# The last product of a chain of matrix products: weights instead of tokens held still in TensorE, and results turned by VectorE

## Chip, cores, metric

One core of a Trainium2 chip. The metric is the device time of one execution in microseconds (us), the median of three runs. A core has TensorE (matrix products, results to PSUM), VectorE, ScalarE and GpSimd (POOL) for elementwise work, SyncE (SP), which issues the DMAs here, and 16 DMA engines between the on-chip memory (SBUF) and the device memory.

## What is computed

Attention with keys and values pooled by 8, and then two blocks of two matrix products each, on 4608 tokens of width 512:

```python
x = attention(q, k, v)                       # 4608 x 512
h = x @ moe_w_in                             # 512 -> 2048
x = np.maximum(0.01 * h, h) @ moe_w_out      # 2048 -> 512
h = x @ moe2_w_in
neg, pos = h <= -1, h >= 1
g = np.where(pos, h, np.where(neg, 0.0, (h + 1) ** 2 / 4))
out = g @ moe2_w_out                         # 4608 x 512
```

Inputs are float32, the weights float64. Each product is made of three TensorE products of a high and a low part (hi x hi, lo x hi, hi x lo).

## The kernel before

There are four stages, one after the other. The first makes the attention and the first product (lines 588 to 590), the second the product with moe_w_out, the third the product with moe2_w_in (line 874), the fourth the product with moe2_w_out. The second and the fourth are two objects of one class, `Blocks`, with `layer` 0 and 1.

`Blocks` multiplies in the manner of Strassen and Winograd: tokens come in pairs of blocks ("pair r": 512 and 512 tokens, the last pair 256 and 256), the 2048 inner columns in two halves, the 512 output columns in two halves, and seven products of sums of blocks replace eight. `ORDER2` is the order of the seven. A **unit** is one of the seven products for one of eight slices f of the inner columns, so there are 5 x 7 x 8 = 280 units: 224 of pairs 0 to 3 and 56 of the last pair. `run` goes through them in order. For unit u it issues

- `unit(u)`: TensorE's matmuls. Layer 0 holds a 128x128 piece of the weights still and moves n tokens (n = 512, in the last pair 256) through it, six matmuls a unit; a result has output columns as its rows (partitions) and tokens along them. Layer 1 holds 128 tokens still and moves 256 columns of the weights, 3 n/128 matmuls a unit; a result has tokens as its rows;
- `hi(u+5)`, ScalarE's copy of the source to the high part (line 1093), and `lo(u+4)`, VectorE's subtraction for the low part (line 1098); the parts lie in six pairs of buffers in turn;
- `g_sum`: the sums of token blocks, on VectorE (line 1078) or, for odd f of the pairs 1 to 3, as an adding DMA issued by POOL (line 1076);
- `g_load`: SP's loads of the next pair (line 1059);
- two steps of `post`, which takes finished products out of PSUM: ScalarE's copies (`snap`, line 1224), VectorE's adds and subtractions (lines 1241 and 1232), POOL's adds (line 1247). A finished block of the result is put on the list `late` with the unit at which SP is to store it (`STORES_LATE` is 6 units on; others 2).

Every engine works through its own instructions in the order in which they were issued, and waits by semaphores. In layer 1 the output tiles of a long pair (`out_tile`) are three rooms, `spare[0]` to `spare[2]`, the fourth tile taking `spare[0]` again. A block of the result, tokens x 256 columns, is stored by one DMA in rows of 1 KB.

In the third stage the weights of the fourth are prepared: `w2_sums` (POOL, lines 785 to 788), `w2_split` (ScalarE line 616, VectorE lines 619 and 621) and a store to device memory.

## Time and profile before

| | |
|---|---|
| time, median of 3 runs | 1664.01 us (1663.68 to 1667.12) |
| profiled execution, its own time | 1663.9 us |
| its span, first to last instruction | 1661.9 us |
| TensorE busy | 1613.5 us, 97% of the span |
| VectorE busy | 1199.9 us, 72% |
| ScalarE busy | 979.3 us, 59% |
| POOL busy | 454.5 us, 27% |
| second stage: first and last matmul start | 576.9 and 929.8 us |
| fourth stage: first and last matmul start | 1291.0 and 1657.6 us |

The profile is of one execution, and the sums below are made against its own time. Busy time is an average over stages with different limits: what a change in one stage is worth is read from that stage, from the wait that ends last there. PE is TensorE, PEld its weight loads, DVE VectorE, ACT ScalarE. Matmuls overlap, so the time of one (the mean) is longer than the distance between two; the busy time of a group divided by its count is the distance.

### The profile page before, as it was taken

Reading aid. Unit: us, or ns where it says so; the run is one execution under the profiler, and the core shown is the slowest. Engines: PE = TensorE matmul, PEld = TensorE weight load, DVE = VectorE, ACT = ScalarE, POOL = GpSimd, SP = SyncE. Lnnn points to the kernel's source line nnn. Section 1 sums busy time; section 2 is a strip of 40 time slices with the busy share of each in tenths; the row PEclk is TensorE's granted clock in tenths of the full one; section 3 lists DMA queues with packets and bytes.
Section 4 is the critical chain, followed back from the end, with each engine's and each line's share of the span. In section 5 each row is a group of like instructions: output and inputs, shape, how many; then the busy total and the mean of one; then the engine's idle time right before and its main releaser. Section 6 shows DMA issues by size and latency. Waiting matters only on the chain.

```text
span 1661.9 us, 28512 instructions
## 1 busy us (share of the span) xinstructions
PE 1613.5 (97%) x9324; PEld 1446.6 (87%) x9324; DVE 1199.9 (72%) x2383; ACT 979.3 (59%) x2113; POOL 454.5 (27%) x572
## 2 busy tenths in 40 slices
PE   6899999999999999999999999999999999999999
PEld 4578787788788888888889999999999999999998
DVE  6858868877855198899898456775673876676767
ACT  4646655556555355666655578887886545454545
POOL 3424333342532003343441111222210013232210
PEclk9999999999999999999999999999999999999999
DMA  7647867678675798899959567557557987777731
GB/s 223 179 142 236 259 225 257 222 237 272 207 231 186 283 364 247 209 280 244 254 148 317 182 223 256 176 195 252 179 199 239 360 269 160 206 156 205 158 117 62
DMA packets 225363, 366.27 MB, mean 220 GB/s; under 512 B 26240, under 2 KB 104064, under 8 KB 225216
## 3 DMA queue, kind: packets, MB, share of 16 engines
q1 hardware_dynamic: 211392, 339.30, 61.3%
q0 software_dynamic: 13824, 25.17, 9.0%
q8 instruction: 73, 1.20, 0.3%
q14 instruction: 74, 0.61, 0.1%
HBM read 196.61 MB, written 142.61 MB: 204 GB/s over the span
## 4 chain that ended last, share of the span: by engine, by line
PE 80%; DVE 10%; ACT 3%; DMA 3%; issue 3%; POOL 1%; SPq 0%; DVEq 0%; ACTq 0%; POOLq 0%
PE u L1135 22%; PE u L1126 20%; PE Y L874 7%; PE h L588 6%; PE h L589 6%; PE h L590 6%; PE X L874 5%; PE V L874 4%; PE sc L432 1%; PE tm L491 1%; DVE vs L338 1%; DVE vr L359 1%; DMA g<-tV 1%; DMA wb0i<-in_moe_w_in_dram 1%; PE av L508 1%
## 5 line engine op out<-in xcount | busy, mean ns | idle before, releaser
L1093 ACT ACTIVATE m<-m 128x512 fp32r<-128x512 f32 (+1 forms) x560 | 328.2, 589 | 320.4 <-PE u L1135 146.8
L1098 DVE TENSOR_TENSOR m<-m,m 128x512 fp32r<-128x512 f32 (+1 forms) x560 | 385.9, 701 | 169.9 <-ACT m L1093 153.1
L1135 PE MATMUL u<-v,m 128*128 128x256 f32 x3024 | 365.1, 284 | 1.7 <-DVE m L1098 1.7
L1135 PEld LDWEIGHTS u<-v,m 128*128 128x128 f32 x3024 | 364.6, 193 | 2.2 <-DVE m L1098 2.1
L1126 PE MATMUL u<-m,v 128*128 128x512 f32 (+1 forms) x1680 | 349.5, 370 | 3.8 <-DVE m L1098 3.6
L1126 PEld LDWEIGHTS u<-m,v 128*128 128x128 f32 x1680 | 294.6, 189 | 58.7 <-DVE m L1098 6.0
L588 PE MATMUL h<-xh,w0i 128*128 128x512 f32 x448 | 184.0, 411 | 0.8 <-ACT t L596 0.8
L589 PE MATMUL h<-xl,w0i 128*128 128x512 f32 x448 | 177.2, 396 | 3.4 <-DVE xl L176 3.4
L590 PE MATMUL h<-xh,w0i 128*128 128x512 f32 x448 | 177.4, 396 | 0.0
L1247 POOL TENSOR_TENSOR o<-o,o 128x512 f32<-128x512 f32 x36 | 63.8, 1799 | 354.2 <-DVE o L1241 352.8
L596 ACT ACTIVATE t<-h 128x512 f32<-128x512 f32 x144 | 86.0, 597 | 122.3 <-PE h L590 67.5
L1078 DVE TENSOR_TENSOR m<-m,m 128x512 f32<-128x512 f32 (+1 forms) x224 | 141.0, 629 | 0.0
L1076 POOL DMA_DIRECT2D m<-m x96 | 84.0, 1036 | 136.4 <-DVE m L1098 108.5
L468 POOL TENSOR_TENSOR at<-at,r 128x32 f32<-128x32 f32 (+3 forms) x160 | 72.3, 473 | 154.9 <-DVE r L465 121.0
L588 PEld LDWEIGHTS h<-xh,w0i 128*128 128x128 f32 x448 | 85.5, 191 | 20.2 <-ACT t L596 1.6
L589 PEld LDWEIGHTS h<-xl,w0i 128*128 128x128 f32 x448 | 85.5, 191 | 19.7 <-DVE xl L176 4.2
L590 PEld LDWEIGHTS h<-xh,w0i 128*128 128x128 f32 x448 | 85.1, 190 | 18.8
L874 PE MATMUL Y<-xs,v 128*128 128x384 f32 x432 | 86.7, 336 | 3.9 <-DVE p L893 3.1
L874 PE MATMUL X<-xs,v 128*128 128x384 f32 x432 | 86.9, 335 | 0.0
L874 PE MATMUL V<-xs,v 128*128 128x384 f32 x432 | 86.5, 334 | 0.0
L874 PEld LDWEIGHTS Y<-xs,v 128*128 128x128 f32 x432 | 75.4, 188 | 6.2 <-DVE p L893 4.1
L874 PEld LDWEIGHTS X<-xs,v 128*128 128x128 f32 x432 | 76.3, 189 | 0.0
(261 smaller groups left out, 2678.9 us busy)
## 6 DMA issues: line engine op xcount, KB each, us to landing
m<-g SPq DMA_DIRECT2D x256, 256.0 KB
g<-t SPq DMA_DIRECT2D x144, 256.0 KB
m<-m POOLq DMA_DIRECT2D x96, 256.0 KB, 5.7
wf<-v0o SPq DMA_DIRECT2D x56, 256.0 KB
wi<-v1i SPq DMA_DIRECT2D x56, 256.0 KB
v<-wf SPq DMA_DIRECT2D x28, 512.0 KB
v<-wi SPq DMA_DIRECT2D x28, 512.0 KB
w2d<-w2o SPq DMA_DIRECT2D x56, 256.0 KB
```

The source lines that it names most:

```text
L468: nc.gpsimd.tensor_tensor(out=t, in0=t, in1=r[0:n].to_broadcast([n, 4, w]), op=ALU.mult)
L588: nc.tensor.matmul(ph, wh[:, c], xh, start=k == 0, stop=False)
L589: nc.tensor.matmul(ph, wh[:, c], xl, start=False, stop=False)
L590: nc.tensor.matmul(ph, wl[:, c], xh, start=False, stop=k == KT - 1)
L596: nc.scalar.activation(out=t, in_=h_t.pop(f), func=AF.Prelu, alpha=0.01)
L874: nc.tensor.matmul(ps, w[:, c], x[k, i], start=begin and k == n == 0, stop=k == 1 and n == 2, skip_group_check=True,)
L1076: nc.gpsimd.dma_start(out=t, in_=x, accum_op=ALU.add)
L1078: nc.vector.tensor_tensor(out=t, in0=x, in1=t, op=ALU.add)
L1093: nc.scalar.activation(out=self.s[u][0], in_=self.unit_source(u), func=AF.Copy)
L1098: nc.vector.tensor_tensor(out=lo, in0=self.unit_source(u), in1=hi, op=ALU.subtract)
L1126: nc.tensor.matmul(banks[b][:, at:at + n], w[:, c], x, start=fresh and at == 0 and i == 0, stop=end and i == 2, skip_group_check=True,)
L1135: nc.tensor.matmul(ps, a[:, c], w, start=fresh and tt % 2 == 0 and i == 0, stop=end and i == 2, skip_group_check=True,)
```

## The change

In layer 1 a unit now has the form of layer 0: a piece of the weights still, n tokens moving. The results come with output columns as rows, and have to be turned before they are stored. VectorE's transpose turns blocks of 32 x 32: block b of 32 tokens and the 32 rows 32a to 32a+31 become 32 rows of tokens. So that the blocks of all four products of a token put together 128 neighbouring output columns in each of the four groups of 32 partitions, the columns are shared out: column 4m + 2e + h of the result is row m of half e of block column h, and `w2_sums` and `w2_split` read the weights in that order (elements 16 bytes apart). `turned` turns a quarter, 256 tokens of one block column, by two instructions into the tile z, in steps of 16 bytes; after the second block column it issues four DMAs, one for each 32 partitions, in pieces of 512 bytes. z has one room, `spare[3]`. The table `TURN` says which quarters are turned when, in units after a block was finished. The fourth output tile takes `spare[1]`.

```diff
--- before.py
+++ after.py
@@ -32,6 +32,10 @@
 UNITS_AHEAD = 10
 EARLY = 12
 STORES_LATE = 6
+TURN = {
+    "r1": (), "r2": (("r1", 0, 2), ("r2", 0, 3), ("r1", 1, 6), ("r2", 1, 7)),
+    "q": (("q", 0, 5),), "c11": (("c11", 0, 0), ("q", 1, 4), ("c11", 1, 4)),
+}
 FIRST = [((2, 1), f) for f in (5, 6, 7)] + [((1, 1), f) for f in range(8)]

 SCORES1 = (-3, -1, 2, 3, 3, 5, 9, 10, 11, 11)
@@ -779,8 +783,10 @@

         def w2_sums(self, f):
             t = self.kept["w2"]
-            b11, b12, b21, b22 = t[:, 0, 0:256], t[:, 0, 256:], t[:, 1, 0:256], t[:, 1, 256:]
-            s = wpool.tile([P, 4, 256], F32, tag=self.spare[1], name=f"w2s{f}")
+            b11, b12, b21, b22 = (
+                t[:, r].rearrange("p (m e h) -> p h e m", e=2, h=2)[:, h] for r in range(2) for h in range(2)
+            )
+            s = wpool.tile([P, 4, 2, P], F32, tag=self.spare[1], name=f"w2s{f}")
             tt = nc.gpsimd.tensor_tensor
             tt(out=s[:, 0], in0=b12, in1=b11, op=ALU.subtract)
             tt(out=s[:, 1], in0=b22, in1=s[:, 0], op=ALU.subtract)
@@ -794,7 +800,8 @@
                     [P, 2, 2, 256], F32R, tag=self.spare[2 + pos // 2 % 2], name=f"w2o{f}_{pos}"
                 )
             t = self.kept["w2o"][:, pos % 2]
-            for _ in signed_split(t[:, 0], t[:, 1], self.kept["w2s"][ORDER2[pos]], ORDER2[pos] < 4):
+            hi, lo = (t[:, i].rearrange("p (e m) -> p e m", e=2) for i in range(2))
+            for _ in signed_split(hi, lo, self.kept["w2s"][ORDER2[pos]], ORDER2[pos] < 4):
                 pass
             nc.sync.dma_start(out=self.w2d[pos][:, f], in_=t.bitcast(F32))

@@ -1118,22 +1125,12 @@
             hi, lo = self.s.pop(u)
             wh, wl = self.w[pos, f]
             fresh, end = prod not in (2, 3) and f == 0, f == self.NJ - 1
-            if self.layer == 0:
-                for e in range(2):
-                    c = slice(e * P, (e + 1) * P)
-                    b, at = divmod(e * n, 512)
-                    for i, (x, w) in enumerate(((hi, wh), (lo, wh), (hi, wl))):
-                        nc.tensor.matmul(
-                            banks[b][:, at:at + n], w[:, c], x, start=fresh and at == 0 and i == 0, stop=end and i == 2,
-                            skip_group_check=True,
-                        )
-                return
-            for tt in range(n // P):
-                c = slice(tt * P, (tt + 1) * P)
-                ps = banks[tt // 2][:, 256 * (tt % 2):256 * (tt % 2) + 256]
-                for i, (a, w) in enumerate(((hi, wh), (hi, wl), (lo, wh))):
+            for e in range(2):
+                c = slice(e * P, (e + 1) * P)
+                b, at = divmod(e * n, 512)
+                for i, (x, w) in enumerate(((hi, wh), (lo, wh), (hi, wl))):
                     nc.tensor.matmul(
-                        ps, a[:, c], w, start=fresh and tt % 2 == 0 and i == 0, stop=end and i == 2,
+                        banks[b][:, at:at + n], w[:, c], x, start=fresh and at == 0 and i == 0, stop=end and i == 2,
                         skip_group_check=True,
                     )

@@ -1175,9 +1172,10 @@
                 if also:
                     also(u)
                 self.now = u
-                while self.late and self.late[0][0] <= u:
-                    _, store, *args = self.late.pop(0)
-                    store(*args)
+                due = [step for step in self.late if step[0] <= u]
+                self.late = [step for step in self.late if step[0] > u]
+                for _, act, *args in due:
+                    act(*args)
                 for step in post[:2]:
                     step()
                 del post[:2]
@@ -1185,8 +1183,8 @@
                     post += self.post(r, prod, self.pair(r)[1])
             for step in post:
                 step()
-            for _, store, *args in self.late:
-                store(*args)
+            for _, act, *args in sorted(self.late, key=lambda step: step[0]):
+                act(*args)

         def out_tile(self, r, i):
             if not self.short(r):
@@ -1207,24 +1205,44 @@

             def store(t, row, col):
                 c = base + (n if row else 0)
+                for e in range(2):
+                    b, at = divmod(e * n, 512)
+                    nc.sync.dma_start(out=x2[2 * col + e][:, c:c + n], in_=t[:, b, at:at + n])
+
+            def turned(key, row, col, part):
+                if key != "c11" and col == (0 if row else 1):
+                    self.kept["z"] = wpool.tile([P, 8, P], F32, tag=self.l2.spare[3], name=f"z{r}_{row}{part}")
+                t, z = self.kept[key, r], self.kept["z"]
+                for e in range(2):
+                    b, at = divmod(e * n + 256 * part, 512)
+                    nc.vector.transpose(
+                        out=z.rearrange("p b (j e h) -> p h e b j", e=2, h=2)[:, col, e],
+                        in_=t[:, b, at:at + 256].rearrange("p (b j) -> p b j", j=32),
+                    )
+                if col == (1 if row else 0):
+                    c = base + (n if row else 0) + 256 * part
+                    for a in range(4):
+                        nc.sync.dma_start(
+                            out=out[c:c + 256, P * a:P * (a + 1)].rearrange("(b i) x -> i b x", i=32),
+                            in_=z[32 * a:32 * a + 32],
+                        )
+
+            def finish(key, row, col, late):
                 if self.layer == 0:
-                    for e in range(2):
-                        b, at = divmod(e * n, 512)
-                        nc.sync.dma_start(out=x2[2 * col + e][:, c:c + n], in_=t[:, b, at:at + n])
+                    self.late.append((self.now + late, store, self.kept[key, r], row, col))
                     return
-                nc.sync.dma_start(
-                    out=out[c:c + n, 256 * col:256 * col + 256].rearrange("(t p) c -> p t c", p=P),
-                    in_=t.rearrange("p b (t c) -> p (b t) c", t=2)[:, 0:n // P],
-                )
+                for k, part, after in TURN[key]:
+                    if part < n // 256:
+                        self.late.append((self.now + after, turned, k, row, int(k in ("r2", "q")), part))

             def snap(key, i, prod, row=None, col=None, scale=1.0):
-                t = self.kept[key, r] = self.out_tile(r, i if self.short(r) else i % 3)
+                t = self.kept[key, r] = self.out_tile(r, i if self.short(r) or i < 3 else 1)
                 yield
                 for k in range(nb):
                     nc.scalar.activation(out=t[:, k], in_=banks(prod)[k], func=AF.Copy, scale=scale)
                     yield
                 if row is not None:
-                    self.late.append((self.now + 2, store, t, row, col))
+                    finish(key, row, col, 2)

             def add_minus(key, prod, row, col):
                 t = self.kept[key, r]
@@ -1233,7 +1251,7 @@
                         out=t[:, k], in0=banks(prod)[k], scalar=-1.0, in1=t[:, k], op0=ALU.mult, op1=ALU.subtract
                     )
                     yield
-                self.late.append((self.now + 2, store, t, row, col))
+                finish(key, row, col, 2)

             def add(key, prod):
                 t = self.kept[key, r]
@@ -1246,7 +1264,7 @@
                 for k in range(nb):
                     nc.gpsimd.tensor_tensor(out=t[:, k], in0=t[:, k], in1=q[:, k], op=ALU.add)
                     yield
-                self.late.append((self.now + STORES_LATE, store, t, row, col))
+                finish(key, row, col, STORES_LATE)

             def chain(*gens):
                 for g in gens:
```

On VectorE the program moves as follows where pair 1 of the fourth stage passes into pair 2 (m are the parts of the tokens, o1r_i the output tiles of pair r, u1r the products in PSUM; zr_rp is z of pair r, block row r and part p). Before:

```order
L1098 TENSOR_TENSOR m1_35_13728<-m1_1_13447,m1_34_13727 128x512
L1098 TENSOR_TENSOR m1_31_13732<-m1_2_13461,m1_30_13731 128x512
L1098 TENSOR_TENSOR m1_29_13749<-m1_3_13477,m1_28_13748 128x512
L1098 TENSOR_TENSOR m1_12_13693<-m1_4_13615,m1_12_13693 128x512
L1232 SCALAR_TENSOR_TENSOR o11_2_15319<-u11_50_14799,o11_2_15319 128x512
L1232 SCALAR_TENSOR_TENSOR o11_2_15319<-u11_51_14800,o11_2_15319 128x512
L1098 TENSOR_TENSOR m1_27_13701<-m1_5_13629,m1_12_13693 128x512
```

and with the change, the same place and what follows:

```order
L1218 STREAM_TRANSPOSE z1_10_14832<-o11_0_14457 128x256 x2
L1105 TENSOR_TENSOR m1_29_13743<-m1_3_13477,m1_28_13742 128x512
L1218 STREAM_TRANSPOSE z1_10_14832<-o11_1_14535 128x256 x2
L1105 TENSOR_TENSOR m1_12_13693<-m1_4_13615,m1_12_13693 128x512
L1250 SCALAR_TENSOR_TENSOR o11_2_14769<-u11_50_14447,o11_2_14769 128x512
L1250 SCALAR_TENSOR_TENSOR o11_2_14769<-u11_51_14448,o11_2_14769 128x512
L1105 TENSOR_TENSOR m1_27_13701<-m1_5_13629,m1_12_13693 128x512
L1105 TENSOR_TENSOR m1_33_13707<-m1_6_13648,m1_32_13706 128x512
L1218 STREAM_TRANSPOSE z1_11_14879<-o11_0_14457 128x256 x2
L1105 TENSOR_TENSOR m1_35_13728<-m1_7_13656,m1_34_13727 128x512
L1218 STREAM_TRANSPOSE z1_11_14879<-o11_1_14535 128x256 x2
```

Two quarters fill z (z1_10), and one quarter of the next fill (z1_11) stands three subtractions of line 1105 and the two of line 1250 behind it. Further on two more fills follow (z1_00 and z1_01), and the second of them stands three subtractions and two sums behind the first.

SP's queue at the same place, before (g2 are the stored tokens, loads of the next pair):

```order
L1059 DMA m1_0_13431<-g2_0_6100 128x512
L1059 DMA m1_1_13447<-g2_1_6101 128x512
L1215 DMA out_dram<-o11_0_14815 128x4x256
L1059 DMA m1_2_13461<-g2_2_6102 128x512
L1215 DMA out_dram<-o11_1_14941 128x4x256
L1059 DMA m1_3_13477<-g2_3_6103 128x512
```

and with the change:

```order
L1225 DMA out_dram<-z1_10_14832 32x8x128 x4
L1066 DMA m1_0_13431<-g2_0_6100 128x512
L1066 DMA m1_1_13447<-g2_1_6101 128x512
L1066 DMA m1_2_13461<-g2_2_6102 128x512
L1066 DMA m1_3_13477<-g2_3_6103 128x512
L1225 DMA out_dram<-z1_11_14879 32x8x128 x4
```

One store of a block's 512 tokens (512 KB) has become two stores of four DMAs for 256 tokens of both block columns, and the loads stand behind the four.

At the end of the program VectorE has two more quarters than before, and SP four DMAs where it had one:

```order
L1105 TENSOR_TENSOR m1_27_13701<-m1_5_13629,m1_12_13693 128x256
L1105 TENSOR_TENSOR m1_33_13707<-m1_6_13648,m1_32_13706 128x256
L1105 TENSOR_TENSOR m1_35_13728<-m1_7_13656,m1_34_13727 128x256
L1218 STREAM_TRANSPOSE z4_00_16616<-o14_2_16502 128x256 x2
L1218 STREAM_TRANSPOSE z4_00_16616<-o14_1_16631 128x256 x2
```

The last row turns the tile that ScalarE copies after the last matmul; before, SP stored that tile itself.

## Rows read from the trace of the kernel before

**Rows 1.** The page's chain that ended last: shares by engine, by line.

```profile
PE 80%; DVE 10%; ACT 3%; DMA 3%; issue 3%; POOL 1%; SPq 0%; DVEq 0%; ACTq 0%; POOLq 0%
PE u L1135 22%; PE u L1126 20%; PE Y L874 7%; PE h L588 6%; PE h L589 6%; PE h L590 6%; PE X L874 5%; PE V L874 4%; PE sc L432 1%; PE tm L491 1%; DVE vs L338 1%; DVE vr L359 1%; DMA g<-tV 1%; DMA wb0i<-in_moe_w_in_dram 1%; PE av L508 1%
```

**Rows 2.** Stretches: length, busy time by engine, granted clock, DMA share, GB/s.

```profile
core 0: us, PE busy (x) PEld busy (x) DVE busy (x) ACT busy (x) POOL busy (x), PEclk, DMA share, GB/s
655.00:733.00 78.00, 78.00 (x346) 64.59 (x345) 71.48 (x119) 48.02 (x90) 33.73 (x33) 1.00 0.83 230
889.00:930.00 41.00, 37.21 (x276) 34.77 (x275) 36.24 (x85) 22.91 (x58) 13.30 (x8) 0.97 0.61 217
930.00:1291.00 361.00, 354.07 (x2018) 349.34 (x2017) 219.96 (x422) 281.97 (x653) 64.00 (x62) 1.00 0.64 219
1291.00:1372.50 81.50, 79.76 (x649) 79.35 (x649) 66.48 (x102) 40.40 (x68) 7.84 (x5) 0.98 0.89 315
1372.50:1453.90 81.40, 81.40 (x680) 81.40 (x680) 55.45 (x81) 39.91 (x65) 20.93 (x20) 1.00 0.75 183
```

**Rows 3.** Waits of the fourth stage, 1291 to 1662: total us, times, longest.

```profile
ACT m L1093 <- PE u L1135: 146.8, 209, 1.1
...
PE u L1135 <- DVE m L1098: 1.7, 1, 1.7
```

**Rows 4.** Second stage's matmuls, 577 to 877 and 884 to 901: count, busy, mean ns.

```profile
L1126 PE MATMUL u<-m,v 128*128 128x512 f32 x1324 | 300.3, 389 | 0.0
...
L1126 PE MATMUL u<-m,v 128*128 128x256 f32 x144 | 17.4, 283 | 0.0
```

**Rows 5.** The fourth stage's matmuls, 1381 to 1611.

```profile
L1135 PE MATMUL u<-v,m 128*128 128x256 f32 x1919 | 230.4, 283 | 0.0
```

**Rows 6.** Timeline at the fourth stage's start: begin, length, what; idle before it.

```profile
1298.47 1.29 DVE L1098 TENSOR_TENSOR m<-m,m 128x512 fp32r<-128x512 f32 x2 [3.00 <-DMA g<-tY]
```

**Rows 7.** Timeline of VectorE and POOL at the end of pair 0.

```profile
1354.63 6.96 POOL L1247 TENSOR_TENSOR o<-o,o 128x512 f32<-128x512 f32 x4 [126.70 <-DVE o L1241]
1354.64 0.69 DVE L1098 TENSOR_TENSOR m<-m,m 128x512 fp32r<-128x512 f32 x1
1355.25 0.68 DVE L1241 TENSOR_TENSOR o<-u,o 128x512 f32<-128x512 f32 x1
...
1358.96 3.19 DVE L1098 TENSOR_TENSOR m<-m,m 128x512 fp32r<-128x512 f32 x2 [0.22 <-ACT m L1093]
```

**Rows 8.** Fourth stage's groups by shape: count, busy us, mean ns, idle before.

```profile
L1093 ACT ACTIVATE m<-m 128x512 fp32r<-128x512 f32 x223 | 140.5, 632 | 162.0 <-PE u L1135 130.1 <-DVE m L1098 18.5 <-ACT o L1224 6.7
...
L1078 DVE TENSOR_TENSOR m<-m,m 128x256 f32<-128x256 f32 x32 | 13.4, 418 | 0.0
```

**Rows 9.** Two reductions of stage one: duration ns min/median/max, first and last start.

```profile
L331 DVE TENSOR_REDUCE ks<-k x28: 722/746/753, 3.7 to 407.4; 128x72 f32<-128x576 f32 x28
...
L338 DVE TENSOR_REDUCE vs<-v x24: 1043/1074/1117, 121.1 to 432.7; 128x64 f32<-128x512 f32 x24
```

**Rows 10.** SP's issues: a 128-partition store, and three 32-partition loads in a row.

```profile
L1215 SPq DMA_DIRECT2D out_dram<-o x20: 372/388/472, 1360.9 to 1658.6; - x20
...
120.69 2.17 SPq L255 DMA_DIRECT2D r<-in_v_dram  x3
```

**Rows 11.** The end: timeline, and SP's last wait for a DMA.

```profile
1657.93 0.60 ACT L1224 ACTIVATE o<-u 128x512 f32<-128x512 f32 x1 [4.07 <-PE u L1135]
1658.55 0.37 SPq L1215 DMA_DIRECT2D out_dram<-o  x1
...
SPq L1435 <- DMA out_dram<-o: 1.6, 1, 1.6
```

**Rows 12.** DMA issues: count, KB each, median us from issue to landing.

```profile
m<-m POOLq DMA_DIRECT2D x96, 256.0 KB, 5.7
```

**Rows 13.** A wait of the second stage, 577 to 930.

```profile
ACT m L1093 <- PE u L1126: 88.9, 138, 2.1
```

**Rows 14.** Third stage's groups on the weights of the fourth, 930 to 1291.

```profile
L616 ACT ACTIVATE w2o<-w2s 128x256 fp32r<-128x256 f32 x32 | 12.3, 411 | 4.7 <-POOL w2s L788 4.7
...
L785 POOL TENSOR_TENSOR w2s<-w2x 128x256 f32<-128x256 f32 x8 | 6.8, 856 | 117.4 <-DMA w2x<-wdo 83.7 <-DVE q L893 33.7
```

## Prediction

> **What bounds the kernel now.** I read the chain that ended last first [rows 1]: TensorE holds 80% of it. The change touches the fourth stage, the units of line 1135, 22% of the chain. The table by stage comes next [rows 2]: from 1372.5 to 1453.9 TensorE is busy in all of 81.40 us, VectorE in 55.45, ScalarE in 39.91. So this stage runs at TensorE's pace, and the waits say so from the other side [rows 3]: ScalarE waits for the units 209 times, a matmul for VectorE once, 1.7 us, at the stage's start.
>
> The second stage does the same work in the form that the change brings here: same units, same buffers, same sums, weights stationary and 512 tokens moving. It is a measurement of the new form. Its matmuls of 512 columns take 300.3 us for 1324, 0.2268 us each [rows 4]; those of 256 columns in the fourth stage take 230.4 us for 1919, 0.1201 each [rows 5]. A unit is six of the first (1.361 us) or twelve of the second (1.441 us). [...]
>
> **The change part by part.**
>
> *TensorE.* 224 of the 280 units (pairs 0 to 3) go from twelve matmuls to six: 224 x 0.080 = 17.9 us less. The 56 units of the last pair, 256 tokens, have six matmuls of 256 before and after: nothing. At the start TensorE waits until VectorE's 1298.47 subtraction, itself released by a DMA of the stage before [rows 6]; the first five units gain nothing, 0.4. **Term 1: -17.5.** [...]
>
> *VectorE, 72 turns.* No row shows a turn. It reads 256 contiguous elements and writes them 16 bytes apart. A subtraction of 512 occupies the engine 0.60 (0.69 long, the next starts 0.61 later [rows 7]), one of 256 0.34 (0.42 long [rows 8], the same 0.08 overlapped). The nearest rows for strides are two reductions to eight-element sums [rows 9]: 576 contiguous elements in 0.746 us, 1.04 ns each over the 0.15 that a subtraction also has; 512 elements read with a stride in 1.074, so 1.81 ns. A turn thus costs between 0.34 (stride free) and 0.53 (256 x 1.81 + 0.15 - 0.08). I take 0.53, the strided row being the nearer; it reads with a stride, the turn writes with one, so 0.34 stays as the other end. [...]
>
> *The one room z.* A quarter is two turns, 1.06 us. Two quarters fill z, four DMAs empty it, and the next fill's first turn waits in VectorE's own order for their landing. Behind it stand the subtractions that TensorE needs. The return: 0.1 to signal, three more issues on SP at 0.44 (0.39 and 0.05 between [rows 10]) to 0.73 (32-partition DMAs, three in 2.17), then 2.1 from the last issue to its landing (1658.55, and SP's wait of 1.6 that begins after it [rows 11]). That is 3.5 to 4.4; I take 3.9 beside the loads of units 48 to 55, 3.5 in the short pair, which loads next to nothing, and 4.6 at a pair's start, where POOL's adding DMAs take 5.7 each [rows 12].
>
> *The reserve.* ScalarE starts on unit u+5 when unit u-1 has ended (six buffers; it waits so 138 times in the second stage [rows 13]), some 0.16 to drain (a matmul of 0.389 at a pitch of 0.227 [rows 4]), 0.63 and 0.69 for the two engines' steps and 0.07 to start them [rows 7, 8], so a subtraction is done some 1.55 us after a unit's start and used at the second matmul five units later: 5 x 1.36 + 0.23 - 1.55, a reserve of about 5.4 us. In the short pair, at 0.72 a unit and 0.42 a step, 2.6.
>
> *A joint between pairs.* While POOL adds, VectorE's subtractions come every 1.70 us instead of every unit [rows 7], four times: it begins the first quarter 1.6 us into unit 46. Unit 10 of the next pair is the first after all eight quarters. Until then VectorE has eight quarters (8.5), sixteen subtractions (9.6), two of line 1232 (1.2), two sums (1.2), and three returns not covered by the work between: 3.9 - 3.0 = 0.9, 3.9 - 1.8 = 2.1, 4.6 - 3.0 = 1.6. Together 25.1. TensorE needs 20 units x 1.36 + 0.2 - 1.6 = 25.8. No stall at the three joints between long pairs, with 0.7 to spare.
>
> At the joint with the short pair TensorE needs only 10 x 1.36 + 10 x 0.72 + 0.1 - 1.6 = 19.3. VectorE has eight quarters (8.5), five long subtractions and line 1232 (4.2), eleven short ones and four or five sums at 0.34 (5.2), and returns of 0.9 + (3.9 - 1.0) + (3.5 - 2.0) = 5.3: 23.2. **Term 2: +3.9**, a stall of TensorE at about unit 10 of the last pair, plus 0.3 for the adds at unit 29, where the reserve is not back. A stall also lowers the clock: 0.98 in the 81.5 us that begin with the wait of rows 3 and 0.97 in 889 to 930, where TensorE stands 3.8 [rows 2], so 1.2 to 1.6 us lost; the new stall is of that size: 0.9. **In all +5.1.** The last pair's own quarters take some of the reserve and end no wait.
>
> *The tail.* Now: ScalarE's copy, one DMA [rows 11]. Then: copy, two turns (1.1), three more issues (1.3 to 2.2, I take 1.8), a landing shorter by some 0.3 since the last DMA carries half the bytes. **Term 3: +2.6.**
>
> *The third stage.* The sums and splits of the weights now read 16 bytes apart: per f four sums on POOL, 0.86 us each, and three of seven splits at 0.41 on ScalarE [rows 14]. ScalarE's first split waits for the fourth sum, 4.7 us in all, while TensorE is busy in 354 of 361 us [rows 2]. At 1.5 times the price the sums end 1.7 later, eight times, in a stage where ScalarE is busy 282 of those 361, so that 1.6 of each 7.3 is free. The bounds are 0 (covered) and 8 (1.0 each time); as most is covered, **term 4: +0.5**.
>
> *Free.* The fourth output tile moves to the second's room, whose earlier reader is done some ten units before. On SP the loads of the next pair now stand behind stores of four DMAs, some 2 us; they are of the product (1,1), first read ten units later.
>
> **Sum.** The profiled execution took 1663.9 (span 1661.9 and 2.0 around), the median 1664.01. 1663.9 - 17.5 + 5.1 + 2.6 + 0.5 = 1654.6.
>
> **The rivals.**
> *Turns cost 0.34.* Eight quarters fall to 5.4, the long joints have room, the stall at the short one is 1.2 or so, the tail 2.2, the third stage 0.5: 1650.3. For it: nothing in a contiguous subtraction's price depends on where it writes. [...]
> *The return is slower.* Three returns a joint: each 0.1 us adds 0.3 to it, once the 0.7 is used. At 0.5 more (4.4 to 5.1) the long joints stall 0.8 each and the short one 5.7: 1658.5; with 0.8 more, 1662. For it: 5.7 for POOL's DMAs [rows 12], and 0.73 for an issue from 32 partitions.
> *Slower than before: z's one room decides.* All but the stalls leaves 13.5. It decides where the four joints stall 13.5 together: 4.2 now, plus 0.3 x 4 per 0.1, less the 0.7 that three of them have to spare, so with returns 0.95 longer than I took (4.5 to 5.6 us). At 1.5 longer the stalls are 4.2 + 4.5 + 3 x 3.8 = 20: 1670. Against it: a store of 256 KB lands in 2.1.
> *The pitch does not fall.* If the 0.227 came from something other than the length, units would keep 1.441: 1663.9 + 3.1 and little stall, 1667.5. Against it: the second stage has weights stationary, and in its short pair 144 matmuls of 256 columns took 17.4 us, 0.121 each [rows 4], as in the fourth stage: the pitch goes with the length. [...]
>
> **Numbers.** As worked out, 1652 to 1657: 0.42. Cheap turns, 1649 to 1652: 0.26. Slower return, 1657 to 1663: 0.19. Beyond it, 1663 to 1675: 0.10. No gain in pitch: 0.03. The likeliest gives 1654.6; the range 1649 to 1663 leaves out some 0.14, nearly all above. What a measurement of this kernel can tell from no change is about 0.2%, 3.3 us: faster means under 1660.7 (the first two cases and 0.11 of the third: 0.79), slower over 1667.3 (0.06 and the last: 0.09), the same between (0.12).
>
> **What would show it.** Step 1: matmuls of the fourth stage at 0.227. Turns: their mean, 0.42 or 0.61 long. z: VectorE waiting for the DMAs of z, three times a pair. Term 2: TensorE waiting for VectorE's subtractions in the last pair, not before it. Tail: from the last matmul to the end 6.6 instead of 4.0. Wrong if TensorE waits at every joint, if turns are longer than 0.7, or if the third stage grows by more than 1 us.

## The result, and the profile after

The changed kernel takes 1679.84 us (median of 6 runs, 1676.27 to 1681.79), the kernel before 1663.85 beside it (6 runs, 1657.88 to 1667.12): 1.0097 of it, 95% interval 1.0076 to 1.0118. It is slower by some 16 us, just under 1% and clear of the interval, where 9 less were forecast. The profiled execution took 1678.7, with a span of 1676.9.

The page's chain that ended last still has TensorE in front, but VectorE's turns, the stores from z and SP's issues of them (line 1225) are on it now, beside VectorE's subtractions (line 1105). It answers to [rows 1].

```profile
PE 69%; DVE 14%; DMA 7%; ACT 4%; issue 3%; SPq 1%; POOL 1%; DVEq 0%; ACTq 0%; POOLq 0%
PE u L1132 34%; PE Y L881 6%; PE h L592 6%; PE h L594 6%; PE h L593 6%; PE X L881 4%; PE V L881 3%; DMA out_dram<-z 2%; DVE m L1105 2%; DVE z L1218 2%; PE sc L436 1%; PE tm L495 1%; SPq L1225 1%; DMA w2d<-w2o 1%; DVE vs L342 1%
```

The table of stretches, cut at the first matmul of the third stage, of the fourth, and of each of its pairs (the last row is the short pair); columns as in [rows 2].

```profile
926.15:1293.04 366.89, 356.54 (x2019) 348.53 (x2017) 226.99 (x422) 288.46 (x653) 67.85 (x62) 1.00 0.63 215
1293.04:1373.94 80.90, 78.48 (x337) 64.01 (x337) 69.80 (x110) 41.70 (x70) 7.74 (x5) 0.98 0.85 295
1373.94:1456.98 83.04, 79.01 (x337) 64.91 (x336) 61.52 (x96) 38.96 (x64) 20.79 (x20) 0.96 0.77 177
1456.98:1541.99 85.01, 79.33 (x338) 65.05 (x336) 61.53 (x96) 38.96 (x64) 20.76 (x20) 0.96 0.76 173
1541.99:1621.81 79.82, 76.48 (x337) 62.96 (x336) 60.35 (x96) 37.79 (x64) 19.89 (x19) 1.00 0.67 152
1621.81:1670.24 48.43, 43.86 (x337) 43.03 (x335) 40.92 (x103) 23.19 (x56) 2.79 (x2) 0.93 0.28 71
```

The matmuls of the fourth stage in a stretch without waits, 1402 to 1470: count, busy us, mean ns.

```profile
L1132 PE MATMUL u<-m,v 128*128 128x512 f32 x302 | 68.6, 389 | 0.0
```

That is 0.227 us each, the pitch of [rows 4]; from one unit's first matmul to the next's it is 1.360 throughout this stretch. A pair of 56 units would take 76.16 us, the short one 40.32. So the stretches above are too long by 4.7 (the stage's start, 3.8 before), **6.9, 8.9, 3.7 and 8.1**. The last four, less the 0.2 that the end had before, make 27.3 us, more than the 17.9 that the shorter units give. The third stage lasts 366.9, where the same bounds give 361.0 before.

The waits of the fourth stage, which answer to [rows 3] (total us, times, longest):

```profile
DVE z L1218 <- DMA out_dram<-z: 38.8, 13, 6.9
...
PE u L1132 <- DVE m L1105: 20.0, 7, 5.7
```

And the timeline at the first joint between pairs (start us, length, engine, what; in brackets the idle time before it):

```profile
1376.10 1.10 DVE L1218 STREAM_TRANSPOSE z<-o 128x256 f32<-128x256 f32 x2 [3.06 <-DMA out_dram<-z]
...
1378.83 0.68 DVE L1085 TENSOR_TENSOR m<-m,m 128x512 f32<-128x512 f32 x1
...
1380.03 1.11 DVE L1218 STREAM_TRANSPOSE z<-o 128x256 f32<-128x256 f32 x2
...
1381.16 14.06 SPq L1225 DMA_DIRECT2D out_dram<-z  x8
1381.56 0.68 DVE L1085 TENSOR_TENSOR m<-m,m 128x512 f32<-128x512 f32 x1
1381.95 3.52 POOL L1083 DMA_DIRECT2D m<-m  x4 [1.88 <-DVE m L1105]
...
1383.35 0.69 DVE L1085 TENSOR_TENSOR m<-m,m 128x512 f32<-128x512 f32 x1
...
1386.84 1.75 POOL L1083 DMA_DIRECT2D m<-m  x2 [1.37 <-DMA m<-m]
1389.40 1.98 DVE L1218 STREAM_TRANSPOSE z<-o 128x256 f32<-128x256 f32 x4 [5.36 <-DMA out_dram<-z]
1391.23 1.26 DVE L1105 TENSOR_TENSOR m<-m,m 128x512 fp32r<-128x512 f32 x2
1391.96 10.13 PEld L1132 LDWEIGHTS u<-m,v 128*128 128x128 f32 x34 [4.46 <-DVE m L1105]
1391.96 10.33 PE L1132 MATMUL u<-m,v 128*128 128x512 f32 x33 [4.03 <-DVE m L1105]
```

Read it from the end. TensorE stands 4.03 us until a subtraction of 1391.23. That one stood in VectorE's order behind the fourth fill's turns, and those waited 5.36 us for z. The third fill ended at 1381.13 (the second turn that begins at 1380.03), its stores were issued from 1381.16 on, and z was free at 1389.40: a return of 8.3 us, while POOL issued its adding DMAs beside it. (A **return** is the time from a fill's last turn to the next fill's first, where that one waits for z; a **joint** is the passage from one pair to the next.) The three returns of a joint are 4.3, 4.8 and 8.3 here; 4.3, 4.8 and 9.8 at the next; 4.3, 5.0 and 7.3 at the third; 4.2, 4.3 and 4.2 at the one with the short pair, whose sums VectorE adds without DMAs.

The tail went as forecast. From the last matmul's end (1670.24) to the end it is 6.7 us; the timeline answers to [rows 11]:

```profile
1670.32 0.60 ACT L1242 ACTIVATE o<-u 128x512 f32<-128x512 f32 x1 [4.43 <-PE u L1132]
1670.95 1.08 DVE L1218 STREAM_TRANSPOSE z<-o 128x256 f32<-128x256 f32 x2 [0.24 <-ACT o L1242]
1672.06 1.84 SPq L1225 DMA_DIRECT2D out_dram<-z  x4
```

By stages, between the two profiled executions: the first two, untouched by the change, 3.9 shorter (over all profiles taken the second stage's first matmul starts anywhere from 573.9 to 579.4); the third 5.9 longer; the fourth 10.4 longer (27.3 + 0.9 at its start - 17.9); the tail 2.6 longer. Together 15.0, the difference of the spans.

### The profile page after: what moved, and what is told of

The parts are those of the page before. It is cut to its first block, busy times and chain, and to the rows that moved or that the text cites. A ratio compares the mean times of both kernels' runs of the same rounds, so it can differ in the third digit from the quotient of the medians.

```text
span 1676.9 us, 25768 instructions
## 1 busy us (share of the span) xinstructions
PE 1604.7 (96%) x7980; PEld 1377.8 (82%) x7980; DVE 1238.3 (74%) x2455; ACT 984.9 (59%) x2113; POOL 457.4 (27%) x572
## 4 chain that ended last, share of the span: by engine, by line
PE 69%; DVE 14%; DMA 7%; ACT 4%; issue 3%; SPq 1%; POOL 1%; DVEq 0%; ACTq 0%; POOLq 0%
PE u L1132 34%; PE Y L881 6%; PE h L592 6%; PE h L594 6%; PE h L593 6%; PE X L881 4%; PE V L881 3%; DMA out_dram<-z 2%; DVE m L1105 2%; DVE z L1218 2%; PE sc L436 1%; PE tm L495 1%; SPq L1225 1%; DMA w2d<-w2o 1%; DVE vs L342 1%
## 5 line engine op out<-in xcount | busy, mean ns | idle before, releaser
L1132 PE MATMUL u<-m,v 128*128 128x512 f32 (+1 forms) x3360 | 705.5, 372 | 23.8 <-DVE m L1105 23.5
L1132 PEld LDWEIGHTS u<-m,v 128*128 128x128 f32 x3360 | 593.6, 191 | 135.7 <-DVE m L1105 28.9
L881 PEld LDWEIGHTS V<-xs,v 128*128 128x128 f32 x432 | 75.7, 188 | 1.8 <-ACT p L894 1.8
L900 DVE TENSOR_TENSOR q<-V,q 128x384 f32<-128x384 f32 x48 | 26.6, 553 | 63.5 <-ACT q L894 63.5
```

The source lines that it names most:

```text
L881: nc.tensor.matmul(ps, w[:, c], x[k, i], start=begin and k == n == 0, stop=k == 1 and n == 2, skip_group_check=True,)
L1132: nc.tensor.matmul(banks[b][:, at:at + n], w[:, c], x, start=fresh and at == 0 and i == 0, stop=end and i == 2, skip_group_check=True,)
```

## Experiments

**Theory.** Two things cost more than the units gave: VectorE standing in line for the one room z, because the third fill's stores come back late beside POOL's adding DMAs; and the third stage's reads 16 bytes apart. **Rivals:** the turns are simply too much work for VectorE at a joint; the next pair's loads, not the adds, hold the stores; the third stage varies by itself.

Below, "joints" are the excess over 1.360 (0.720) us a unit at the start of pairs 1 to 4, read as above; "long" are those between pairs of 512 and 512 tokens. In the changed kernel the three long ones come to 19.4 together, the short one to 7.5 up to its unit 14 (of the 8.1 above, 0.5 come at its unit 50 and 0.2 at the end).

**1. The weight reads undone.**

```diff
-            b11, b12, b21, b22 = (t[:, r].rearrange("p (m e h) -> p h e m", e=2, h=2)[:, h] ...)
+            b11, b12, b21, b22 = t[:, 0, 0:256], t[:, 0, 256:], t[:, 1, 0:256], t[:, 1, 256:]
...
-            for _ in signed_split(hi, lo, self.kept["w2s"][ORDER2[pos]], ORDER2[pos] < 4):
+            for _ in signed_split(t[:, 0], t[:, 1], self.kept["w2s"][ORDER2[pos]], ORDER2[pos] < 4):
```

> The changed kernel with the sums and splits of the last weights reading contiguous columns again, as in the kernel before; the output's columns come out in another order within each four. In the changed kernel's trace the third stage (first matmul of the first phase to the first unit of the last stage) lasts 366.9 us, 5.9 more than before. Theory (the 16-byte reads cost it): splits of w2x fall from 657 ns back to about 411, the third stage to about 361, the time from 1679.8 to about 1674. Rival (the third stage varies from run to run by that much, the reads are covered): splits get cheaper, the time stays at 1678 to 1681.

This run takes 1674.7 us (1669.73 to 1677.37), 1.0078 of the kernel before (1.0058 to 1.0098), and its third stage 361.8. First the third stage's groups on these weights in the changed kernel (count, busy us, mean ns, idle before), then those of this run:

```profile
L620 ACT ACTIVATE w2o<-w2x 128x256 fp32r<-128x256 f32 x24 | 15.8, 657 | 2.8 <-DMA w2d<-w2o 2.5 <-DVE q L900 0.3
L623 DVE SCALAR_TENSOR_TENSOR w2o<-w2x,w2o 128x256 fp32r<-128x256 f32 x24 | 14.9, 621 | 5.8 <-ACT w2o L620 5.5
...
L793 POOL TENSOR_TENSOR w2s<-w2x 128x256 f32<-128x256 f32 x8 | 9.6, 1206 | 0.0
```

```profile
L623 DVE SCALAR_TENSOR_TENSOR w2o<-w2x,w2o 128x256 fp32r<-128x256 f32 x24 | 10.2, 423 | 2.3 <-ACT w2o L620 1.6 <-DMA w2d<-w2o 0.5
L620 ACT ACTIVATE w2o<-w2x 128x256 fp32r<-128x256 f32 x24 | 9.9, 411 | 1.9 <-DMA w2d<-w2o 1.9
...
L791 POOL TENSOR_TENSOR w2s<-w2x 128x256 f32<-128x256 f32 x8 | 6.2, 776 | 0.0
```

A split that reads 16 bytes apart costs ScalarE 246 ns more and VectorE 198 more. On POOL the third sum costs 430 more, but all four sums together only 465. With contiguous reads the stage is back at its old length.

**2. The other way round: the kernel before with these reads alone** (the hunks of `w2_sums` and `w2_split` from the change).

> The kernel before with the 16-byte weight reads of the third stage alone; its output's columns come out in another order within each four. Theory (these reads cost 6 to 8 us by themselves): third stage 367 to 369, 1669 to 1672, 1.0035 to 1.005 of the kernel before. Rival (they cost only together with what the change does at the stage's end): third stage 361 to 363, within 2 us of the kernel before.

It takes 1671.22 us (1668.25 to 1674.27), 1.0051 (1.0034 to 1.0068), and its third stage 368.0. The reads cost that stage its time by themselves. Over all profiles taken, the third stage lasts 366.9 to 369.6 in the eight kernels with reads 16 bytes apart, and 360.1 to 361.8 in the five others with contiguous ones (the kernel before, runs 1 and 9, and the two of 10): some 7 us.

**3. The new matmul form alone.**

```diff
+            def plain(t, row, col):
...
-                for k, part, after in TURN[key]:
-                    if part < n // 256:
-                        self.late.append((self.now + after, turned, k, row, int(k in ("r2", "q")), part))
+                self.late.append((self.now + late, plain, self.kept[key, r], row, col))
```

> The changed kernel without turns and without z: the output tiles are stored as they are by one DMA each, in the places and at the times of the kernel before, so the output is not turned. This is the new matmul form alone, with the 16-byte weight reads. Theory (all that the fourth stage lost came with turns and z): units stay at 1.360 us, the joints' 27 us of excess go, the tail falls from 6.7 to about 4: 1648 to 1652. Rival (longer matmuls bring a stall of their own, by ScalarE or VectorE getting less time a unit): TensorE still waits for subtractions at the joints, over 1656.

It takes 1653.52 us (1651.15 to 1655.72), 0.9954 (0.9937 to 0.997), 1.5 over the expected range: the third stage took 368.8, the fourth's start 1.4 more than before. (That start is the same work in all kernels of the new form, and its excess varies from 2.4 to 6.4 between their profiles.) The fourth stage took 350.3 after 366.8, with no excess at any joint, and the tail was 4.1. So the gain of the form is there, and all that the joints lost came with the turns and z.

**4. POOL's adding DMAs left out of the last stage.**

```diff
             if by_dma:
-                nc.gpsimd.dma_start(out=t, in_=x, accum_op=ALU.add)
+                if self.layer == 0:
+                    nc.gpsimd.dma_start(out=t, in_=x, accum_op=ALU.add)
```

> The changed kernel with POOL's 48 adding DMAs of the last stage left out (these sums are missing from the result). Theory (the third fill's stores land late because they stand behind the adding DMAs): the return after the third fill falls from 8.3, 9.8 and 7.3 us to 4.2 to 5, the three joints between long pairs lose nearly all of their 19 us: about 1660 to 1664. Rival (the next pair's loads on SP hold the stores, or the stores are slow of themselves): the returns stay over 7 us, the time within 4 us of 1680.

It takes 1660.66 us (1658.86 to 1663.26), 0.9994 (0.9985 to 1.0004). The returns after a third fill are 4.2, 4.5 and 4.1, the long joints 0.0, 0.1 and 0.0; the short one keeps 6.4. The DMA queues, first of the changed kernel from 1381 to 1392, then of this run from 1382 to 1393, each the 11 us about the landing of a third fill (packets, MB, share of 16 engines):

```profile
q0 software_dynamic: 844, 1.55, 81.8%
q1 hardware_dynamic: 1088, 0.52, 24.5%
```

```profile
q1 hardware_dynamic: 1723, 1.01, 38.5%
```

With the adding DMAs (q0) the 16 engines are full for all of this time (shares of 81.8% and 24.5%, together over 100%). SP's queue (q1), which carries the stores and the loads, moves 0.52 MB in it, no more than the fill itself (512 KB), so no load was left to hold the stores; and the loads that SP issues are in both runs. The rival of the loads falls. A return of 8.3 us in place of 4.3 is mostly landing: the four issues took 2.5 us in place of the first fill's 1.9, and from there to z being free it was 5.7 in place of 2.4. Whether stores in pieces larger than 512 bytes would return sooner beside the adds, no run shows. A store beside the adds was slowed, not shut out: the third fills came back among them, after 7.3 to 9.8 us in place of 4.1 to 4.5.

**5. The same turns, given out over more units.**

```diff
+SPREAD = {
+    "r1": (), "r2": (("r1", 0, 2), ("r2", 0, 3), ("r1", 1, 8), ("r2", 1, 9)),
+    "q": (("q", 0, 9),), "c11": (("c11", 0, 2), ("q", 1, 10), ("c11", 1, 11)),
+}
...
-                for k, part, after in TURN[key]:
+                for k, part, after in (SPREAD if n > 256 else TURN)[key]:
```

> The changed kernel with the turns of the four long pairs given out later: the second fill of z starts 6 units after the first, the third 6 after that, the fourth 9 after the third; same turns, same stores, same one room. Theory (VectorE stands in line behind z's landing, above all behind the third fill's, which came back after 7.3 to 9.8 us): the waits for z in front of turns go from 38.8 us to under 10, the excess of units 9 to 14 at the three joints between long pairs (6.9, 8.9 and 3.7 us over 1.36 a unit, clock included) goes, that at the short pair (7.5) falls: 1653 to 1661. Rival (eight quarters are more work than VectorE can do beside the subtractions at a joint, the wait only shows it): TensorE stalls later, the time stays within 4 us of 1680.

It takes 1663.24 us (1655.97 to 1664.94), 1.0001 (0.9988 to 1.0014): 16.6 better than the changed kernel, but short of the expected range. The joints fell to 1.9, 3.9, 1.5 and 1.4, and VectorE still waited 27.6 us for z: the second fill's stores, six units later, now stood among the adds (returns of 7.7 to 8.3 in place of 4.8), and the third's took 13.2 to 13.6. The work had not become less, so the rival of too much work falls; but moving a store into the adding DMAs lengthened its return.

**6. Later only where the adds end.**

```diff
+LONG = {
+    "r1": (), "r2": TURN["r2"], "q": (("q", 0, 9),), "c11": (("c11", 0, 2), ("q", 1, 13), ("c11", 1, 13)),
+}
...
+                for k, part, after in (LONG, LONG, LONG, LAST_LONG, TURN)[r][key]:
```

(LAST_LONG is the spread table of the run above.)

> The changed kernel with the first two fills of z at their own times, the third 4 units later and the fourth 13 units after the last store of a pair's fourth tile, so that the third fill's stores have some 14 us to land while POOL's adding DMAs run; at the joint with the short pair the times of the run that spread them. Theory (what is left of the spread run's 8.7 us is the wait for a return of 13 us that starts amid the adding DMAs): turns wait under 2 us for z at the long joints, their excess falls from 7.3 to under 1: 1654 to 1659 with the third stage as slow as in the changed kernel. Rival (returns there grow with whatever is given them, the queue never drains before unit 22): excess stays over 5, 1661 to 1665.

It takes 1656.18 us (1651.9 to 1660.02), 0.996 (0.9946 to 0.9975). The long joints have no excess, the short one 1.4. From the third fill's end to the fourth's first turn there are now 13.2 us at all three, and no turn waits in between. Waits of this run from 1285 to 1655:

```profile
DVE z L1225 <- DMA out_dram<-z: 5.9, 5, 1.6
...
PE u L1139 <- DVE m L1112: 2.8, 4, 1.7
```

**7. A second room for z.**

```diff
-                    self.kept["z"] = wpool.tile([P, 8, P], F32, tag=self.l2.spare[3], name=f"z{r}_{row}{part}")
+                    self.n_z = getattr(self, "n_z", 0) + 1
+                    if self.n_z % 2:
+                        zs = [wpool.tile([P, 8, P], F32, tag=self.l2.spare[3], name=f"z{r}_{row}{part}")]
+                    else:
+                        zs = [raw_p.tile([P, 4, P], F32, tag="raw", name=f"z{r}_{row}{part}{i}") for i in range(2)]
...
```

> The changed kernel with a second room for z: every second fill goes into two tiles of half the size that the last stage doesn't use otherwise (so eight turns of 128 columns in place of four of 256 in such a fill, and eight DMAs). Times of the turns, weights and sums as in the changed kernel. Theory (one room, and VectorE in line behind its landing): no wait of a turn for z over 1 us, excess of the joints between long pairs from 19.4 us to under 3, of the short one from 7.5 to under 3.5, the third stage stays at 367 to 369: 1655 to 1660. Rival (VectorE has too much work at a joint): the joints keep more than 8 us, over 1664.

It takes 1656.05 us (1654.27 to 1660.45), 0.9968 (0.9956 to 0.998). No turn waits for z, at the changed kernel's own times and with 36 more turns; joints 0.0, 0.0, 0.0 and 0.5, tail 7.7. The wait was for the room.

**8. Turns that write contiguously.**

```diff
-                        out=z.rearrange("p b (j e h) -> p h e b j", e=2, h=2)[:, col, e],
+                        out=z.rearrange("p (h e b) j -> p h e (b j)", h=2, e=2, b=2)[:, col, e].rearrange("p (b j) -> p b j", j=32),
```

> The changed kernel with turns that write 256 elements one behind another in z, in place of 16 bytes apart; the output's values come out in other places. Theory (the write's stride costs nothing or next to it): a turn stays at 0.46 to 0.50 us from one start to the next, 0.60 to 0.62 long; waits and time as in the changed kernel, 1676 to 1682. Rival (the stride is what lifts it over a contiguous operation of 256): 0.34 from start to start, 0.42 long, and the joints' excess some 4 to 6 us lower.

It takes 1671.15 us (2 runs, 1668.23 and 1674.08), 1.0053 (1.0032 to 1.0073). The theory of this run fell, its rival was right. The turns of the changed kernel, then of this run (ns, least, median, most; first and last start):

```profile
L1218 DVE STREAM_TRANSPOSE z<-o x72: 594/615/654, 1361.9 to 1671.4; 128x256 f32<-128x256 f32 x72
```

```profile
L1218 DVE STREAM_TRANSPOSE z<-o x72: 395/404/447, 1363.9 to 1666.9; 128x256 f32<-128x256 f32 x72
```

From one start to the next it is 0.33 to 0.37 us in place of 0.44 to 0.50. The short joint went from 7.5 to 4.3, the long ones only from 19.4 to 16.7 together: VectorE gave out the third fill's stores earlier, they returned after 11.4, 9.2 and 10.0 us, and it waited longer (43.6 us for z in all).

The contiguous turn, 404 ns, took about as long as a subtraction of 256 elements, 418 [rows 8]; the one that writes 16 bytes apart, 615, took half as long again.

**9. The weights put in order one stage earlier.** The columns are sorted by POOL's 32 additions of the second stage and by the loads of the third.

```diff
+        if key[:2] == (1, "o"):
+            w_f32[key, part] = ef
+            inner = [x.rearrange("p (m c) -> p c m", c=4) for x in (a, lo)]
+            nc.gpsimd.tensor_tensor(out=e.rearrange("p (c m) -> p c m", c=4), in0=inner[0], in1=inner[1], op=ALU.add)
...
```

> The changed kernel with the weights' columns put in their order in the second stage, in POOL's 32 additions of line 646 (it idles there two thirds of the time), and in the load of the third; sums and splits of the third stage read contiguous columns, the result is the reference's. Theory (the 16-byte reads cost the third stage 6 to 8 us): the third stage falls to 361 to 363, the second stays at 352 to 353, 1672 to 1675. Rival (the cost moves with the strides): the second stage grows by over 2 us and the time stays over 1677.

It takes 1674.57 us (1670.93 to 1678.42), 1.0073 (1.0059 to 1.0088). In this run the output's columns still come out in another order within each four. The third stage takes 360.9, the second 351.9 as in the changed kernel: POOL's additions went from 1034 to 1338 ns and nothing waited for them.

**10. Both cures together**, with the columns' order of run 9 set right: later fills, and two rooms.

> The later fills of one of the runs (third fill 4 units later, fourth 13 after) together with the weights' columns put in order in the second stage (POOL's additions of line 646). Theory (the two causes are apart and add up): third stage 361 to 362, no excess at the long joints: 1648 to 1652, 0.99 to 0.994 of the kernel before. Rival (one of the gains is undone by the other, or by the second stage): over 1654.

> Two rooms for z, with the fills at the changed kernel's times, together with the weights' columns put in order in the second stage. Theory: third stage 361 to 362, joints as in the run with two rooms, the tail of that run (7.7): 1648 to 1652. Rival as for the run beside it: over 1654.

With later fills it takes 1651.65 us (1648.74 to 1654.6), 0.9934 (0.9917 to 0.9952), with two rooms 1650.73 (1647.8 to 1655.04), 0.9929 (0.9911 to 0.9947). Both beat the kernel before, by 0.7%, and the changed one. The third and fourth stage of the run with later fills, as stretches:

```profile
930.40:1290.50 360.10, 353.80 (x2019) 349.10 (x2017) 219.51 (x422) 281.97 (x653) 62.84 (x62) 1.00 0.65 219
1290.50:1639.90 349.40, 346.58 (x1681) 292.45 (x1680) 293.28 (x501) 181.23 (x318) 72.00 (x66) 1.00 0.74 197
```

## Why the prediction was wrong, point by point

**Term 1, -17.5: right.** The unit measures 1.360 us against 1.361 forecast, and the form alone took 16.5 off the fourth stage (run 3), with a start that was 1.4 longer. In the changed kernel the start was 0.9 longer, so 17.0 were left of the 17.9. In this stream, with a weight load for each matmul, the pitch was 0.227 us for 512 columns, and 0.120 for 256 in the kernel before, both at a granted clock of 1.00.

**The turn, 0.53: between its two ends.** It measured 0.44 to 0.50 from start to start, mostly 0.46, and 0.615 long. Writes 16 bytes apart do cost: 0.12 of the distance and 0.21 of the length (run 8). The argument for 0.34 held only as far as the rows went, for contiguous subtractions: 0.69 long into m, 0.68 into o [rows 7].

**The return, 3.9, 3.9 and 4.6: this step failed.** The sentence was "4.6 at a pair's start, where POOL's adding DMAs take 5.7 each". I added 0.7 to a landing read at the end of the kernel, when the queues are empty (a DMA share of 0.00 from 1655 to 1658 before the change); beside adding DMAs that fill the engines (81.8% of them for q0 alone from 1381 to 1392) the return took 7.3 to 9.8. The 0.1 to signal, part of all three, stood on no row, and no run shows it by itself; in the timeline the first issue began 0.03 after the fill had ended (1381.13 and 1381.16). The arithmetic around it came out within 0.3. With the measured returns, the first joint's 4.3 + 4.8 + 8.3 is 5.0 more than I took, less the 0.7 to spare: a wait of 4.3, where TensorE stood 4.03. The second gives 5.8 (5.68 measured), the third 3.5 (3.34). That it is so close is in part luck: the sixteen turns of a joint took about 1.1 less than the 8.5, and three sums stood before unit 10 (1378.83, 1381.56 and 1383.35 in the timeline) where I had two, 0.6 more. At the short joint the 3.9 forecast at about unit 10 measured 3.72, and that is luck too: its returns were 1.4 longer together than the 11.3 I took, its turns 1.1 shorter. The 0.3 at unit 29 did not come, 0.62 at unit 3 did, and 0.5 at unit 50, at the last pair's own quarters, which I had put at nothing (runs 3 and 8 don't have it). The rival that ended on the other side, "z's one room decides", named the one room as the cause; runs 4, 6 and 7 show it. It took all three returns to be 0.95 to 1.5 longer, where the first two were 0.4 to 1.1 longer and the third 2.7 to 5.2. It had a chance of 0.10, for 1663 to 1675; the time lies above even that, by the clock and the third stage.

**The clock, 0.9: mis-sized too.** TensorE's waits for VectorE from the first joint on come to 17.6 us of the 27.3 (the 20.0 above less 2.4 at the start); the other 9.7 are mostly units at a lower clock after them, some 3 us at each of three joints (6.9 less 4.03, 8.9 less 5.68, 7.5 less 4.34), where 0.9 was taken for the one stall forecast. The changed kernel's stretches, in which the granted clock is the column before the last two:

```profile
1390.00:1400.00 10.00, 8.04 (x24) 6.49 (x25) 9.18 (x17) 3.53 (x6) 2.58 (x3) 0.66 1.07 190
1470.00:1480.00 10.00, 4.32 (x13) 3.15 (x12) 5.92 (x11) 1.94 (x4) 3.33 (x4) 0.80 1.00 180
1480.00:1490.00 10.00, 10.00 (x39) 8.08 (x39) 7.39 (x13) 4.77 (x9) 0.99 (x2) 0.86 0.92 215
1550.00:1560.00 10.00, 6.66 (x30) 5.21 (x29) 5.61 (x12) 2.90 (x5) 5.27 (x6) 1.00 1.07 195
1630.00:1640.00 10.00, 6.28 (x31) 6.08 (x31) 8.16 (x23) 3.29 (x8) 0.00 (x0) 0.66 0.40 95
```

After TensorE's waits of 4.03, 5.68 and 3.72 the granted clock was 0.50 for some us (1394.3 to 1396.8, 1478.9 to 1481.5, 1634 to 1638): a unit that takes 1.36 at a granted clock of 1.00 took 2.56, one of the short pair 1.28 in place of 0.72. After the wait of 3.34 the clock stayed at 1.00, and that joint lost only 0.3 beyond its wait. The length of the wait alone does not tell which it will be: in run 8 the granted clock was 0.54 after a wait of 3.38 (1478.3 to 1480.6) and 1.00 after one of 3.46 (1559 to 1564).

**Term 3, +2.6: right.** From the last matmul to the end it took 6.7, where 6.6 was forecast. One of its parts no run shows: the 0.3 by which I took the landing shorter for half the bytes stood on no row, and from the end of the last issue to the end of the span it was 3.0 before and after (1658.92 to 1661.9, 1673.90 to 1676.9). The three more issues made up for it, 1.5 in place of 1.8.

**Term 4, +0.5: failed too.** The price of the reads was right (the slope of [rows 9] gives 0.20 more for 256 elements; VectorE's splits cost 0.198 more, ScalarE's 0.246). For POOL's sums the factor 1.5, which no row gave, did not come: the four took 0.47 us more per f, not 1.7, so the later sums that I priced are at most part of the cost. What failed was "as most is covered": the stage grew by 5.9 in this profile and about 7 over all, near the upper bound of 8. I counted ScalarE's splits and POOL's sums, not VectorE's splits, and it is VectorE's additions of line 900 that TensorE waits for in that stage (8.2 us in 10 waits, 6.1 in 6 before). In the one profile of the changed kernel TensorE's idle time in that stage is 10.4 us after 6.9; where the rest of the growth sits is not settled.

**The sum.** With the measured sizes, on the profiled execution before: 1663.9 - 17.0 + 27.3 + 2.6 + 5.9 = 1682.7, and 1678.8 less the first two stages' 3.9; measured 1678.7. Of the three signs of being wrong that I had named, TensorE waiting at every joint and a third stage longer by more than 1 us came; turns longer than 0.7 did not.

## What to carry to other kernels

Price a transfer's return where it will run, beside what the queues carry at that moment: here z was free 2.4 us after the last issue of a first fill's stores, and 5.7 after that of a third fill's, amid the adds. VectorE, which runs its work in order, passed its wait on (behind its 5.36 us for z TensorE stood 4.03), so give a buffer that is refilled early either a second room or a refill time after the slowest return (1656.05 and 1656.18 us, where it was 1679.84). When a layout trick moves strides into another stage, put them on an engine that nobody waits for there: the same sort cost 7 us in the third stage and nothing that shows on POOL in the second and in the third stage's loads.

## What was new about the hardware

A store of 512 KB in four DMAs came back in 4.1 to 4.5 us without adding DMAs beside it, and in 7.3 to 13.6 amid them. A 128x256 turn on VectorE took 404 ns writing contiguously and 615 ns writing 16 bytes apart. Waits of TensorE of 3.34 and 3.46 us left the granted clock at 1.00, others of 3.38 and of 3.72 to 5.68 were followed by 0.50 to 0.54.
